# A fused attention and sine-gated feed-forward kernel on one Trainium2 core: the hand-held order of its 1816 steps is drawn up anew

## The chip, the cores and the metric

One core of one Trainium2 chip. The metric is the device time of one execution in microseconds (us), 381.02 as the median of three runs before the change (379.35, 381.02, 384.81). The engines are called by the profile's names: PE (TensorE; PEld its weight loads), ACT (ScalarE), DVE (VectorE), POOL (GpSimd) and SP (SyncE), which only issues transfers.

## The reference

Eight batches of eight heads, 576 positions of 64 values; then a feed-forward over the 4608 rows of 512.

```python
scores = q @ k.T / sqrt(64) + bias[bucket(|i - j|), head]
attn = exp(scores - max) / (sum + 1e-9)
x = (attn @ v).transpose(0, 2, 1, 3).reshape(4608, 512)
h = x @ w_in                       # 512 -> 2048
s = sin(alpha * h)
out = (h + s * s / (alpha + 1e-9)) @ w_out   # 2048 -> 512
```

## The kernel before, in words

The work is cut into 1816 named steps by `_graph` (L46 on), each with the engines that it may run on, what it depends on, how many of the eight PSUM banks it takes and which later steps free them. The text `ORDER` (from L343) lists all steps; `_planned` walks it, checks it and hands each step to an engine. Every engine runs its own steps in the order of that text and waits by semaphore for what a step needs. So the text alone sets each engine's queue, the banks and the choice of engine. A word is a step, then a slash with an engine's letter where it isn't the first choice (A ACT, D DVE, G POOL) and the bank number.

The names, with t a batch (0 to 7), p a pair of heads (0 to 3), b a block of 512 rows (0 to 8), f a 128-wide part of the 2048, and tau a tile of 128 output rows:

- `n` loads rows of q or k in fp16 on POOL (L581) and `t`, `c` turn them on PE (L703) and copy them (L653, L651), for batches 0 to 2. From batch 3 on `g` stages them in DRAM through POOL (L608) and `k` turns them with a transposing transfer on SP (L614).
- `v`, `y` load the value rows on POOL (L587, L593). For batch t they wait until every product with the values of batch t-2 is done, since two sets of buffers are used in turn.
- `T` is a score group of four matmuls (L766), `X..q`, `X..r` and `S` the scores of the last 64 positions (L749, L720, L725); `E..` is the exp on ACT (L774, L734) and `B..` the multiplication by the exp of the bias on DVE (L797, L779, L783, L740). There are 13 buffers for exps of `T` and 4 for those of `X`.
- `A` and `L` are the products with the values (L805, L810, L821); `N` and `NL` divide by the sums on DVE (L842, L843); `Y` and `YL` turn the result into the feed-forward's input xT, by PE for batch 0 (`P`, L868) and else by a transposing transfer on SP (L850, L861).
- `I` is the first feed-forward product, four 512-wide matmuls (L887), `Z` its sine on ACT (L893), `Q` the square on DVE or ACT (L900, L898), `G` the gate on DVE (L905), `O` two 512-wide matmuls of the second product (L915; the last tile goes in halves), `W` the eviction on DVE or ACT (L653, L651) and `D` the store on SP or ACT (L928).
- `j`, `m` load the bias pattern (L662, on SP or POOL) and cut its masks (L668, on POOL or DVE).

Block b's first product needs `Y` of all pairs of every batch that its rows touch. The order mixes batch t+1's attention with block t's feed-forward, so that PE has matmuls while ACT does exps. After the last exp, PE has some 20 us of `O` left.

Of the kernel before, what the change touches and what calls it, by code (L numbers as in the profile page):

```python
# [14 lines left out]
T, H, S, D = 8, 8, 576, 64  # L15
# [340 lines left out]
ET1100 P03/5 Y01 t120/4 BT1011 t210/7 ET1300 T1010/0 c120 L0/6 ET1010 Y03 wo0 t230/4 NL0 t200/5
T1311/2 c200 T1301/0 I0.8/6 ET1311 c230 ET1301 S1/5 c210 X11r/2 v10 I0.0/4 BT1000 EX11r BT1100 v13
I0.3/7 ES1 Z0.0 BS1 BT1010 I0.9/5 BT1300 PL0/3 I0.7/2 YL0 n211 Z0.9 Q0.0 I0.1/3 wo1 Z0.3 Q0.9 G0.0
Z0.7 I0.12/1 v21 Q0.3/A G0.9 I0.2/4 wo2 Z0.8 G0.3 Q0.7/A I0.5/5 n201 Q0.8 Z0.2 G0.7 I0.14/7 Z0.1
Q0.2 Q0.1/A G0.8 I0.10/2 Z0.12 wo3 G0.2 I0.13/6 Q0.12/A BX10r g31 G0.1 Z0.10 I0.4/4 BT1001 Z0.14  # L360
G0.12 A100/3 Q0.10/A Q0.14 I0.11/1 Z0.5 G0.10 g30 Z0.4 G0.14 I0.6/0 Q0.4/A BX11r Z0.11 N100
I0.15/7 G0.4 Q0.5/A y20 O0.0/3 Z0.6 G0.5 O1.0/2 g40 Q0.6/A O0.2 O0.4 Z0.15 G0.6 T1101/4 Z0.13 O1.2
Q0.11 ET1101 Q0.15 O0.6 G0.11 v22 A101/0 BT1301 O0.8 G0.15 A130/1 N101 O1.4 N130 Y10 O1.6 Q0.13
X11q/4 T1111/0 G0.13 t211/7 v20 ET1111 O1.8 c211 O0.10 y21 EX11q BT1111 T1200/0 O1.10 BT1311
ET1200 t201/7 t221/6 T1110/4 c221 T1201/0 ET1110 O1.12 BT1200 O1.14 ET1201 c201 O0.12 T1310/4 v23
W1 X10q/6 ET1310 T1210/0 BT1101 O0.14 BT1110 BX11q A110/2 BT1201 EX10q W0 A111/5 BT1310 D0 ET1210
N110 A120/4 N111 T1211/6 T2100/2 o2 T2110/0 ET1211 Y11 O3.0/5 BT1210 BX10q O3.2 ET2100 BT1211 O3.4
# [4 lines left out]
I1.1/7 Z1.5 g71 A210/6 I1.14/1 N210 Z1.8 NL1 I1.15/0 y31 Q1.8/A Q1.5 I1.0/6 G1.5 Z1.14 g50 Z1.1  # L372
I1.2/5 Q1.14 G1.8 Z1.0 I1.7/3 Q1.0/A BT2110 G1.14 v30 A220/2 G1.0 Z1.7 I1.13/1 g41 Q1.1/A N220
Z1.2 I1.6/6 G1.1 Q1.7/A Q1.2 I1.4/2 o3/A G1.7 Z1.6 I1.3/7 BT2000 Z1.4 G1.2 O2.12 Z1.15 O2.14 Q1.4
Q1.6/A I1.10/5 G1.4 g51 W2/A Q1.15 O5.0/3 Z1.3 G1.6 I1.12/4 Q1.3/A G1.15 Z1.13 I1.9/6 G1.3 Z1.10
O6.0/2 Q1.13 Z1.12 I1.11/7 G1.13 Z1.9 Q1.10 g60 X21q/0 Q1.9 Z1.11 O5.2 G1.10 EX21q O6.2 Q1.11 O5.4
BT2210 G1.9 A211/5 O5.6 G1.11 O6.4 BT2211 T2011/6 T2300/0 Q1.12 O6.6 ET2300 G1.12 O5.8 O6.8 N211
ET2011 O6.10 BT2010 Y21 BT2300 T2301/0 T2311/4 BT2011 T3110/6 O6.12 ET2311 BT2310 O5.10 BT2001
ET2301 O5.12 D2 O6.14 A200/5 ET3110 BT2301 O5.14 N200 W6/A T3300/0 YL1 T3011/6 W5 X20q/4 ET3300
# [601 lines left out]
```

## Time and profile before

| what | value |
|---|---|
| median of three runs | 381.02 us |
| the profiled execution | 381.76 us |
| its span, first to last instruction | 379.9 us |
| matmuls of PE | 3769 |
| first matmul starts | 3.85 us |

The profile's page gives the busy time of each engine, the span in 40 slices of 9.5 us (a digit is tenths; PEclk is the clock that TensorE was granted), and the chain of work that ended last. Of a row of stretches, the columns are its bounds, its length, the busy time of PE, PEld, DVE, ACT and POOL with counts, the granted clock, the DMA share and GB/s; where one engine alone was asked for, its busy time stands alone. A timeline row has the start, how long a merged piece lasts, the engine, line and operation, and in brackets the idle time before it with who ended it. A row of waits has the sum, the count and the longest. A matmul's own duration includes its latency; consecutive ones overlap, so a cost is read from starts.

### The profile page before, as it was taken

Reading aid. Unit: us, or ns where it says so; the run is one execution under the profiler, and the core shown is the slowest. Engines: PE = TensorE matmul, PEld = TensorE weight load, DVE = VectorE, ACT = ScalarE, POOL = GpSimd, SP = SyncE. Lnnn points to the kernel's source line nnn. Section 1 sums busy time; section 2 is a strip of 40 time slices with the busy share of each in tenths; the row PEclk is TensorE's granted clock in tenths of the full one; section 3 lists DMA queues with packets and bytes.
Section 4 is the critical chain, followed back from the end, with each engine's and each line's share of the span. In section 5 each row is a group of like instructions: output and inputs, shape, how many; then the busy total and the mean of one; then the engine's idle time right before and its main releaser. Section 6 shows DMA issues by size and latency. Waiting matters only on the chain.

```text
span 379.9 us, 9143 instructions
## 1 busy us (share of the span) xinstructions
PE 365.4 (96%) x3769; PEld 195.6 (51%) x3769; DVE 265.3 (70%) x613; ACT 310.5 (82%) x417; POOL 86.0 (23%) x104
## 2 busy tenths in 40 slices
PE   4879999999998899999999999999999999999996
PEld 3567445654464455544554555445654564444453
DVE  4789899639975496389754985596729866769412
ACT  5979998999899599899988989999899855686301
POOL 8894682048208000600000050500000000000000
PEclk9989999999999899999999999999999999999999
DMA  9999999999999992890254078980130032020005
GB/s 174 217 170 184 186 193 158 126 201 145 157 131 142 172 100 57 93 155 21 98 129 97 0 83 135 141 69 28 40 89 3 2 83 92 2 83 0 2 29 193
DMA packets 140889, 39.68 MB, mean 104 GB/s; under 512 B 126208, under 2 KB 136304, under 8 KB 140848
## 3 DMA queue, kind: packets, MB, share of 16 engines
q0 software_dynamic: 92864, 18.45, 60.0%
q1 hardware_dynamic: 46272, 18.61, 23.5%
q10 hardware_dynamic: 1712, 2.04, 1.6%
q8 instruction: 29, 0.48, 0.5%
q14 instruction: 12, 0.10, 0.1%
HBM read 36.89 MB, written 15.34 MB: 137 GB/s over the span
## 4 chain that ended last, share of the span: by engine, by line
PE 88%; DMA 6%; ACT 2%; POOL 1%; issue 1%; SPq 1%; DVE 1%; POOLq 0%
PE acc L915 33%; PE acc L887 31%; PE acc L810 8%; PE acc L766 8%; PE acc L805 2%; DMA xT<-xp 2%; DMA v<-in_v_dram 2%; PE acc L821 2%; DMA xT<-in_k_dram 2%; DMA toep<-e_sb 1%; ACT s L893 1%; PE acc L720 1%; PE acc L703 1%; POOL xT L581 1%; PE acc L749 1%
## 5 line engine op out<-in xcount | busy, mean ns | idle before, releaser
L915 PE MATMUL acc<-w_out,g 128*128 128x512 f16 (+1 forms) x592 | 144.3, 374 | 0.0
L887 PE MATMUL acc<-xT,w_in 128*128 128x512 f16 x576 | 135.8, 381 | 2.8 <-DMA xT<-xp 2.2
L774 ACT ACTIVATE u<-acc 128x1024 f16<-128x1024 f32 x128 | 123.7, 1034 | 12.2 <-PE acc L766 11.3
L893 ACT ACTIVATE s<-acc,alphaT 128x512 f16<-128x512 f32 x144 | 91.9, 682 | 23.6 <-PE acc L887 23.0
L905 DVE SCALAR_TENSOR_TENSOR g<-s,inv_a,acc 128x512 f16<-128x512 f16 x144 | 103.2, 742 | 7.3 <-ACT s L898 5.7
L887 PEld LDWEIGHTS <-w_in 128*128 128x128 f16 x576 | 55.3, 98 | 69.2 <-issue 6.5
L915 PEld LDWEIGHTS <-g 128*128 128x128 f16 x592 | 52.7, 98 | 59.0 <-issue 7.3
L797 DVE TENSOR_TENSOR u<-u,toep 128x256 f16<-128x256 f16 (+1 forms) x128 | 58.9, 489 | 19.8 <-ACT u L774 19.5
L587 POOL DMA_DIRECT2D v<-in_v_dram x32 | 30.9, 972 | 145.5 <-PE acc L821 79.0
L810 PE MATMUL acc<-v,u 128*128 128x65 f16 x1024 | 45.4, 196 | 0.5 <-DMA v<-in_v_dram 0.5
L900 DVE TENSOR_TENSOR s<-s 128x512 f16<-128x512 f16 x83 | 34.0, 419 | 17.0 <-ACT s L893 16.7
L810 PEld LDWEIGHTS <-u 128*128 128x128 f16 x1024 | 41.9, 99 | 4.9 <-issue 0.9
L766 PE MATMUL acc<-qT,kT 64*128 64x256 f16 x512 | 42.0, 278 | 1.5 <-DVE kT L653 1.0
L898 ACT ACTIVATE s<-s 128x512 f16<-128x512 f16 x61 | 37.9, 629 | 1.1
L653 DVE COPY outs<-acc 128x512 f32<-128x512 f32 (+1 forms) x24 | 16.2, 675 | 26.7 <-PE acc L915 25.4
L774 ACT ACTIVATE ux<-acc 128x1024 f16<-128x1024 f32 x32 | 32.4, 1035 | 1.8 <-PE acc L720 0.9
L766 PEld LDWEIGHTS <-kT 64*128 64x128 f16 x512 | 20.4, 96 | 22.8 <-issue 18.2
L842 DVE RECIPROCAL rden<-acc 128x4 f32<-128x4 f32 x72 | 12.7, 177 | 25.1 <-PE acc L810 18.7
L805 PE MATMUL acc<-vt,ux 128*128 128x130 f16 x128 | 28.8, 225 | 1.0 <-DMA vt<-in_v_dram 1.0
L843 DVE TENSOR_TENSOR xp<-acc,rden 128x256 f16<-128x256 f32 x64 | 27.2, 424 | 2.3
L651 ACT ACTIVATE outs<-acc 128x512 f32<-128x512 f32 (+1 forms) x13 | 7.6, 582 | 18.6 <-PE acc L915 18.5
L805 PEld LDWEIGHTS <-ux 128*128 128x128 f16 x128 | 12.7, 99 | 8.2 <-issue 2.8
(68 smaller groups left out, 199.2 us busy)
## 6 DMA issues: line engine op xcount, KB each, us to landing
out_dram<-outs SPq DMA_DIRECT2D x30, 256.0 KB, 2.3
v<-in_v_dram POOLq DMA_DIRECT2D x32, 128.0 KB, 6.8
staged_q<-in_q_dram POOLq DMA_DIRECT2D x5, 576.0 KB, 12.4
staged_k<-in_k_dram POOLq DMA_DIRECT2D x5, 576.0 KB, 14.9
w_in<-in_moe_w_in_dram POOLq DMA_DIRECT2D x4, 512.0 KB, 10.5
w_out<-in_moe_w_out_dram POOLq DMA_DIRECT2D x4, 512.0 KB, 10.6
xT<-in_q_dram POOLq DMA_DIRECT2D x11, 144.0 KB, 5.6
xT<-in_k_dram POOLq DMA_DIRECT2D x11, 144.0 KB, 5.9
```

Of the source, the lines that this page charges most:

```text
L587: self.nc.gpsimd.dma_start(out=self.vs[t % 2][:, c, :, 0:D], in_=src)
L766: self.nc.tensor.matmul(out=s[:, o:o + 256], lhsT=self.kT[t % 2][r, p, 128 * c:128 * c + 128], rhs=self.qT[t % 2][r, p, 256 * w:256 * w + ...
L774: self.nc.scalar.activation(out=c["u"], in_=c["s"], func=AF.Exp, scale=0.125)
L797: self.nc.vector.tensor_tensor(out=io, in0=io, in1=m, op=ALU.mult)
L805: nc.tensor.matmul(out=c["av"][:, 130 * j:130 * j + 130], lhsT=cx["u"][:, o:o + 128], rhs=vt[:, p, :], start=True, stop=True, skip_group_c ...
L810: nc.tensor.matmul(out=c["av"][:, 130 * j + 65 * a:130 * j + 65 * a + 65], lhsT=cells[ch // 2]["u"][:, o:o + 128], rhs=vv[:, ch, 2 * p + a ...
L887: self.nc.tensor.matmul(out=c["h"], lhsT=self.w_in[:, j, 128 * f:128 * f + 128], rhs=self.xT[:, j, 512 * b:512 * b + 512], start=(j == 0), ...
L893: self.nc.scalar.activation(out=c["s"], in_=c["h"], func=AF.Sin, scale=self.alphaT[:, f:f + 1])
L898: self.nc.scalar.activation(out=c["s"], in_=c["s"], func=AF.Square)
L900: self.nc.vector.tensor_tensor(out=c["s"], in0=c["s"], in1=c["s"], op=ALU.mult)
L905: self.nc.vector.scalar_tensor_tensor(out=self.g[b][:, f, :], in0=c["s"], scalar=self.inv_a[:, f:f + 1], in1=c["h"], op0=ALU.mult, op1=ALU ...
L915: self.nc.tensor.matmul(out=c["mo"], lhsT=self.g[b][:, f, 128 * (tau % 4):128 * (tau % 4) + 128], rhs=self.w_out[:, f, at], start=(f == 0) ...
```

## The change

The text `ORDER` is replaced; no other line differs, and each of the 1816 steps occurs in both. [...] What differs: the order on every engine, the banks, and some choices of engine. 44 squares go from DVE to ACT and 34 from ACT to DVE (on ACT 61 before, 71 after); of the evictions 10 go to ACT and 9 away (13 before, 14 after); stores on ACT's queue are 9 instead of 7; mask m0 goes from POOL to DVE; a few copies change sides. The table of ACT is changed between exp and sine 16 times in both. Core of the diff, with the places around the first product with values (A000), block 1's first product (I1.5, then I1.11) and block 2's (I2.0, then I2.14):

```diff
 ORDER = """
-id/A r00 ms r10/A r01 n011 r11/A sub n020 cst tab al n021 n100 f00 n031 th00/7 f10/A ch00 n010 f01
-th10/6 y00 th01/7 ch10 ch01/A T0000/0 v00 T0001/2 ET0000 n131 bu/7 ET0001 f11 t020/6 n030 be
...
-T0311/6 BX00r EX01q BT0011 A000/3 n210 BT0300 A010/2 EX00q n220 N000 A001/5 m3 BT0211 ET0311
...
-X20r/6 N120 ET2110 A131/3 S2/4 A121/2 EX20r N131 T2200/0 N121 O3.6 ES2 ET2200 BT2100 T2111/6 Y12
-T2101/2 O2.0/4 ET2111 O3.8 X21r/0 ET2101 O3.10 Y13 O3.12 EX21r O3.14 T2000/2 k30 T2201/6 T2211/0
-ET2000 O2.2 O2.4 ET2201 O2.6 O2.8 ET2211 BT2201 O2.10 BT2101 W3 T2001/2 T2210/6 T2010/0 BT2111
-ET2001 D3 L1/5 BT2200 ET2010 I1.5/3 BX21r D1 v33 BX20r ET2210 T2310/0 v32 k31 I1.8/2 ET2310 y30
...
-A221/2 BS2 BT2311 O4.0/3 EX20q N221 O4.2 BT3300 T3301/0 ET3011 T3000/4 Y22 A201/2 BX21q ET3301
...
-X31q/0 v31 T3111/4 O7.2 ET3111 Y20 g70 O7.4 O4.14 EX31q X30q/4 W4 T3201/6 O7.6 EX30q BT3011 k41
-S3/3 O7.8 g61 BT3000 ET3201 O7.10 BT3110 X31r/0 BX30r BX31q T3200/4 ES3 BT3001 EX31r T3010/6
-BT3111 I2.0/3 BT3201 v43 ET3010 A300/1 I2.14/0 ET3200 BT3010 BT3301 N300 I2.5/7 Z2.0 D6 BT3101
...
+id/A r00 ms r10/A r01 n011 r11/A sub n020 cst tab al n021 n010 f00 n030 th00/7 f10/A ch00 n131 f01
+th10/6 n031 th01/7 ch10/A ch01 T0000/0 y01 T0001/2 ET0000 t011/7 n100 f11/A bu/6 c011 v02 t020/5
...
+BT0101 t101/6 n200 ET0210 c110 T0311/0 T0110/4 n120 c101 A000/7 ET0311 m3 BT0210 A001/6 N000
...
+N121 T2311/4 EX21r T2211/6 BT2201 Y12 A131/1 BX11q ET2211 O3.10 N131 X21q/2 ET2311 T2100/6 Y13
+L1/1 EX21q O3.12 NL1 v32 k31 ET2100 O3.14 T2000/2 v20 W3 T2110/4 ET2000 T2101/6 S2/1 BT2211 v31
+I1.11/0 BT2311 ET2110 I1.12/3 g30 BT2210 BX21q ET2101 BT2300 D1 I1.9/2 BT2110 BX21r ES2 BT2200
...
+T3110/4 A201/6 Y21 ET3111 T3301/2 ET3110 v42 X30q/0 BT3111 O7.0/7 BT3010 g50 ET3301 O7.2 N201 O7.4
+BT3001 Y20 BX30r X31r/4 EX30q BT3110 BT3201 O4.0/6 BT3100 O7.6 EX31r T3300/0 D6 v41 T3210/2 ET3300
+T3101/4 g61 O4.2 ET3101 O4.4 BT3300 O7.8 BT3200 X31q/0 ET3210 T3011/4 O7.10 v43 ET3011 I2.14/3
...
 """
```

SP's queue around block 2 is, before: k30 D3 D1 k31 Y21 D2 YL1 Y22 k40 Y23 YL2 Y20 k41 D6; and after: D1 k30 D3 Y23 D0 Y22 YL1 k40 k41 D5 Y21 Y20 D6. POOL's queue begins, before, with 18 transfers of n, y, v and j ahead of v02, the last of batch 0's values; after, with 19 ahead of v01, the last there.

More of the change, by code (lines that the diff above doesn't have):

```diff
@@ L356 @@
[L356 to L367, printed above, removed]
@@ L374 @@
[L374 to L379, printed above, removed]
@@ new lines @@
+t131/6 c030 X00r/4 ET0111 n101 t100/1 c131 v00 t111/7 EX00r X00q/2 c111 v03 EX00q c100 T0211/4
+T0101/6 v01 m0/D ET0101 T0201/0 BT0011 X01r/2 n121 BT0111 ET0211 n201 BT0100 T0310/6 EX01r m1
+BT0000 t130/5 n231 ET0310 BX00r S0/4 BT0200 m2 T0210/2 c130 ET0201 wi1 t110/7 BT0010 BT0001 ES0
+BT0101 t101/6 n200 ET0210 c110 T0311/0 T0110/4 n120 c101 A000/7 ET0311 m3 BT0210 A001/6 N000
+ET0110 v12 T0301/0 N001 T0300/2 t121/7 ET0301 wi0 BT0310 X01q/4 BT0201 BX01r A010/6 BT0110 ET0300
+y11 BT0311 A020/1 n230 N010 EX01q A011/0 n220 BT0211 T1011/2 c121/A N011 T1100/4 A031/6 ET1011
@@ new lines @@
+O0.12 ET1211 W1 O0.14 X11q/0 ET2300 W0 t211/5 t210/3 A130/4 EX11q c210 T1310/6 BX10q T2210/2
+c211/A N130 A111/1 ET2210 BT1210 O3.0/0 N111 T2301/4 ET1310 T2201/2 BT1311 Y11 O3.2 BT1211 ET2301
+O3.4 A120/1 ET2201 BT2301 T2310/4 o2 T2200/6 O3.6 N120 ET2310 X21r/2 BT1310 A121/1 ET2200 O3.8
+N121 T2311/4 EX21r T2211/6 BT2201 Y12 A131/1 BX11q ET2211 O3.10 N131 X21q/2 ET2311 T2100/6 Y13
+L1/1 EX21q O3.12 NL1 v32 k31 ET2100 O3.14 T2000/2 v20 W3 T2110/4 ET2000 T2101/6 S2/1 BT2211 v31
+I1.11/0 BT2311 ET2110 I1.12/3 g30 BT2210 BX21q ET2101 BT2300 D1 I1.9/2 BT2110 BX21r ES2 BT2200
@@ new lines @@
+Z1.12 I1.6/7 y31 I1.1/6 v33 I1.8/1 Z1.1 Q1.12 v30 Z1.6 I1.5/5 Q1.1 g40 G1.12 Q1.6/A I1.14/4 Z1.5
+G1.1 Q1.5/A O2.0/3 BT2101 G1.6 O2.2 Z1.8 A220/6 BS2 y30 Z1.11 G1.5 I1.10/7 Q1.11/A Q1.8 N220
+I1.4/5 Z1.10 G1.11 Z1.14 O2.4 G1.8 I1.3/6 Q1.10/A BT2100 Z1.9 I1.0/1 Q1.14 Z1.3 G1.10 I1.13/0
+Q1.3/A k30 Q1.9 G1.14 I1.7/7 Z1.13 BT2310 G1.9 Z1.0 O2.6 G1.3 A230/4 Q1.13/A I1.2/2 Q1.0/A G1.13
+Z1.4 N230 I1.15/6 Z1.7 Q1.4 Z1.2 O2.8 G1.0 A231/4 Q1.2/A G1.4 D3 O2.10 Z1.15 N231 O2.12 Q1.15/A
+O6.0/5 G1.2 Q1.7/A X20r/0 O5.0/4 G1.7 EX20r A221/2 Y23 G1.15 O2.14 O6.2 N221 O6.4 W2 X20q/6 D0
@@ new lines @@
+T2011/0 T2001/2 EX20q O5.2 Y22 O6.6 ET2011 BX20q O5.4 O6.8 ET2001 o3 T2111/0 YL1 T2010/6 O5.6
+ET2010 L2/3 ET2111 X30r/6 NL2 k40 O6.10 EX30r BX20r T3201/0 BT2011 T3000/2 O6.12 BT2010 ET3000
+BT2111 O6.14 T3010/6 ET3201 BT3000 T3001/2 O5.8 k41 BT2001 ET3010 O5.10 W6 O5.12 BT2000 A210/5
+ET3001 O5.14 N210 S3/7 T3200/0 ES3 W5 T3100/2 A211/6 ET3200 BS3 D5 A200/7 ET3100 N211 T3111/0 N200
+T3110/4 A201/6 Y21 ET3111 T3301/2 ET3110 v42 X30q/0 BT3111 O7.0/7 BT3010 g50 ET3301 O7.2 N201 O7.4
+BT3001 Y20 BX30r X31r/4 EX30q BT3110 BT3201 O4.0/6 BT3100 O7.6 EX31r T3300/0 D6 v41 T3210/2 ET3300
@@ new lines @@
+A311/3 N310 Z2.8 X41r/0 O4.12 N311 EX41r O4.14 G2.6 O9.0/4 BT3301 O9.2 W4 O9.4 Q2.8 T3311/2 D4
+BX30q T3310/6 G2.8 A320/1 ET3311 BX31q YL2 O8.0/5 ET3310 N320 O8.2 S4/0 O8.4 ES4 BT3310 T3211/2
+T4000/0 T4301/6 ET3211 O9.6 Y31 O9.8 ET4000 O9.10 A330/3 ET4301 O8.6 N330 T4001/0 T4310/6 BT3211
+T4200/2 ET4001 O9.12 BT3311 O9.14 ET4200 A321/1 W9 O8.8 ET4310 N321 D9 T4300/2 T4311/0 ET4300
+T4011/6 A331/4 Y32 ET4011 O8.10 N331 O8.12 ET4311 BT4200 T4210/2 Y33 T4201/6 BT4011 L3/4 ET4201
+BT4000 T4211/0 k50 y51 ET4210 NL3 T4010/6 O8.14 v53 ET4211 X40r/2 I3.11/4 y41 ET4010 BT4211 y40
@@ L460 @@
+O31.10 O34.4 O33.8 O30.14 O29.8 W30 O28.10 O33.10 D30/A O31.12 O31.14 O28.12 W31 O35.0b/4 O34.6
+D31/A O35.0a/6 O34.8 O28.14 O35.4b W28 O35.8b O33.12 D28 O34.10 O29.10 O35.12b O29.12 W35b/A O32.6
+D35b O33.14 O29.14 W33 O32.8 W29/A O32.10 D33 D29/A O34.12 O32.12 O34.14 O32.14 W34/A O35.4a D34/A
+W32 O35.8a O35.12a D32 W35a/A D35a/A
 """
```

166 lines of the change are left out of this document (79 added, 87 removed).

## The prediction

> **What bounds the kernel now.** I read the page first, then the waits of TensorE, then the stretches around its two stalls.
>
> ```profile
> PE 365.4 (96%) x3769; PEld 195.6 (51%) x3769; DVE 265.3 (70%) x613; ACT 310.5 (82%) x417; POOL 86.0 (23%) x104
> ...
> PEclk9989999999999899999999999999999999999999
> DMA  9999999999999992890254078980130032020005
> ...
> PE 88%; DMA 6%; ACT 2%; POOL 1%; issue 1%; SPq 1%; DVE 1%; POOLq 0%
> ```
> ```profile
> PE acc L887 <- DMA xT<-xp: 2.2, 1, 2.2
> PE acc L805 <- DMA vt<-in_v_dram: 1.0, 1, 1.0
> PE acc L766 <- DVE kT L653: 1.0, 2, 0.8
> ...
> PE acc L887 <- issue: 0.6, 1, 0.6
> PE acc L810 <- DMA v<-in_v_dram: 0.5, 1, 0.5
> ```
> ```profile
> 122.00:125.00 3.00, 0.84 (x10) 0.42 (x9) 1.49 (x5) 2.98 (x5) 1.82 (x2) 1.00 1.38 108
> 125.00:128.50 3.50, 3.50 (x26) 1.99 (x24) 1.17 (x4) 1.88 (x2) 0.00 (x0) 0.51 1.74 128
> ...
> 19.20:22.70 3.50, 1.44 (x43) 0.95 (x43) 3.50 (x9) 3.50 (x5) 3.33 (x8) 1.00 1.45 175
> 22.70:26.10 3.40, 3.40 (x61) 3.31 (x61) 2.52 (x7) 1.23 (x2) 3.23 (x7) 0.50 1.14 158
> ```
>
> TensorE is busy 96% of the span and carries 88% of the chain. The change neither adds nor removes a product, so it can only win back stalls, and these are small: the five waits above sum to 5.3 us. Two stand for most of what can be moved. At 122 us TensorE is idle for 2.2 us (0.84 busy of 3.00) and in the next 3.5 us its clock is 0.51, which loses another 0.49 x 3.5 = 1.7: 3.9 us at one place. Around 21 us it waits for the value rows (1.0 + 0.5), and 3.4 us at clock 0.50 follow: 1.7 more.
>
> **Part 1, the order of the transposed rows on SyncE (-3.6 us).** Why was the transposed row late at 122 us?
>
> ```profile
> 110.01 1.19 SPq L850 DMA_TRANSPOSE xT<-xp  x1
> 111.31 2.98 SPq L614 DMA_TRANSPOSE kT<-staged_k  x1
> 114.38 1.22 SPq L850 DMA_TRANSPOSE xT<-xp  x1
> 115.70 2.46 SPq L861 DMA_TRANSPOSE xT<-xl  x2
> 118.21 1.26 SPq L850 DMA_TRANSPOSE xT<-xp  x1
> 119.57 4.58 SPq L614 DMA_TRANSPOSE qT<-staged_q  x1
> ```
> ```profile
> L850 SPq DMA_TRANSPOSE xT<-xp x28: 1188/1206/2107, 59.6 to 311.6; - x28
> ...
> DMA to landing us min/median/max: 2.4/2.5/7.3
> ```
> ```profile
> L842 DVE RECIPROCAL rden<-acc 128x4 f32<-128x4 f32 x72 | 12.7, 177 | 25.1 <-PE acc L810 18.7
> L843 DVE TENSOR_TENSOR xp<-acc,rden 128x256 f16<-128x256 f32 x64 | 27.2, 424 | 2.3
> ```
> ```profile
> 124.66 1.50 PE L887 MATMUL acc<-xT,w_in 128*128 128x512 f16 x4 [2.16 <-DMA xT<-xp]
> ```
> The piece of 118.21 is Y20, which I2.0 waits for. Ahead of it on SyncE stood the transposes k40, Y23 and YL2; and where the median landing is 2.5 us after the issue, I2.0 could start only at 124.66, 6.4 after it. In the new order k40 and k41 stand well ahead, and only Y21 stands between them and Y20. From the last product by v (A201) to the first product of block 2 (now I2.14) TensorE has 9 moe-out pieces (18 matmuls), 5 score groups, two X..q and one X..r group. Their prices:
>
> ```profile
> 342.00:361.00 19.00, 19.00 (x89) 8.60 (x88) 13.10 (x25) 9.40 (x16) 0.00 (x0) 1.00 0.00 1
> ...
> 20.09 0.41 PE L749 MATMUL acc<-qT,kT 64*128 64x64 f16 x16 [0.29 <-DVE qT L653]
> ...
> 28.69 0.39 PE L766 MATMUL acc<-qT,kT 64*128 64x256 f16 x4
> 29.01 0.31 PE L725 MATMUL acc<-qT,kT 64*64 64x64 f16 x8
> 29.25 0.70 PE L703 MATMUL acc<-ident,xT 96*64 96x96 f16 x24
> ```
> ```profile
> 80.27 0.74 PE acc L821 x34
> ```
> A 128x512 matmul costs 19.00/89 = 0.213; a score group 0.32 (28.69 to 29.01); an X..q 0.41; an X..r two 512-wide matmuls, 0.43. Sum 18 x 0.213 + 5 x 0.32 + 0.82 + 0.43 = 6.7 us of cover. Against it: 0.177 + 0.424 for the division plus some 0.1 to start, then 2.5 (quiet) to 7.3 (worst): 3.2 to 8.0. I take 7.0, near the slow end, because k41 and the first of batch 4's loads may overlap it: a stall of 0.3, and no slow clock. Gain 3.6; bounds 3.9 and, at 8.0 (idle 1.3), 2.6 or, if the clock then falls, 0.9.
>
> **Part 2, the same cover elsewhere (+0.5 us).** The new order cuts it. Block 1 begins 3.7 us after A131 (3 moe-out pieces 1.28, 4 score groups 1.28, X21q 0.41, L1 0.74, and S2, four matmuls of 64 columns) where before 8.7 us lay between A121 and I1.5. Priced alike, the shortest covers of blocks 3 to 7 go from 8.2, 5.2, 5.6, 6.1, 4.8 to 3.7, 3.9, 4.4, 4.3, 4.6. The need on a quiet queue is 3.2, or 4.4 where another transpose's 1.2 of issue stands just ahead. So each holds by a hair: I charge some 0.1 a block, 0.5 in all. Ends: 0, and for a landing of 7.3 at block 1 an idle time of 4.3 and a slow stretch of 1.7.
>
> **Part 3, the head (-0.4 us).**
>
> ```profile
> 21.76 0.23 PE L805 MATMUL acc<-vt,ux 128*128 128x130 f16 x1 [1.04 <-DMA vt<-in_v_dram]
> ...
> 22.59 0.45 PE L810 MATMUL acc<-v,u 128*128 128x65 f16 x6 [0.54 <-DMA v<-in_v_dram]
> ```
> ```profile
> L581 POOL DMA_DIRECT2D xT<-in_q_dram x11 | 7.3, 661 | 1.7 <-POOLq L965 0.8 <-DMA w_in<-in_moe_w_in_dram 0.6
> ...
> L668 POOL COPY mt<-toep 64x192 f16<-64x192 f16 x8 | 3.1, 388 | 0.3
> ```
> A000 starts when the last of batch 0's value rows lands, 22.6 before. It is now the 20th load on GpSimd's queue and was the 19th, by one row load: up to 0.66 later. In the wait TensorE now does more ahead of A000: one score group, S0 (0.31) and two turns (0.70) more, X01q (0.41) less: 0.9 us. Net -0.9 to +0.5 with the rest unmoved; I take -0.4. Mask m0 goes to VectorE, 2 x 0.39 by GpSimd's row; the value rows cover it, and if they land earlier it is paid once, 0.8. The slow clock at 22.7 I leave: TensorE is still idle more than half of the stretch ahead of it.
>
> **Part 4, ScalarE and VectorE (+0.5 us).**
>
> ```profile
> L774 ACT ACTIVATE u<-acc 128x1024 f16<-128x1024 f32 x128 | 123.7, 1034 | 12.2 <-PE acc L766 11.3
> L893 ACT ACTIVATE s<-acc,alphaT 128x512 f16<-128x512 f32 x144 | 91.9, 682 | 23.6 <-PE acc L887 23.0
> ...
> L900 DVE TENSOR_TENSOR s<-s 128x512 f16<-128x512 f16 x83 | 34.0, 419 | 17.0 <-ACT s L893 16.7
> ...
> L898 ACT ACTIVATE s<-s 128x512 f16<-128x512 f16 x61 | 37.9, 629 | 1.1
> ```
> ```profile
> 90.00:100.00 10.00, 9.91 (x18) 1.00 2.45 157
> ```
> Squares on ScalarE go from 61 to 71: 10 x 0.629 = 6.3 us more there, 10 x 0.419 = 4.2 less on VectorE. Over the span both have room (82% and 70%), so TensorE's work hides it; but until about 120 us ScalarE is nearly full (9.91 of 10.00). Counted in the written order from block 0's first product to block 2's, ScalarE's work is now 95% of TensorE's and was 92%. Score groups whose banks wait for an exp stand with less behind them, so a few waits of some tenths come: I take 0.5, bounds 0 and 3. Evictions (13 to 14 on ScalarE) and two stores moved to its queue cost nothing beside the last block's matmuls; without that cover, one eviction. Table loads stay at 16. Value loads of batches 2, 4 and 5 now stand behind loads that wait for an older batch's last product; counted by their order each still lands 3 us or more ahead of its use, and a lost cover is paid one for one.
>
> **Sum.** -3.6 + 0.5 - 0.4 + 0.5 = -3.0. The profiled execution took 381.76 (span 379.9 and 1.9 around it), so 378.8. That execution stands 0.7 above the median of the runs shown, 381.02, which range from 379.35 to 384.81. Faster or slower by under 2% of the median (373.4 to 388.6) is about what a measurement of this kernel can tell from no change, so I forecast no change that counts.
>
> **Rivals.** (a) My sum: 378.8, by itself 376 to 381. Chance 0.45.
> (b) Slower: the cut cover fails at block 1. The worst landing, 7.3, with 0.7 ahead of it makes 8.0 against 3.7: 4.3 idle and 1.7 of slow clock instead of the 0.1 charged, 378.8 + 5.9 = 384.7. It is slower than before from an extra loss of 3.0, that is from a landing of 4.4 or more with the slow clock. For it: SyncE's landings spread from 2.4 to 7.3, and block 1 falls in the first 145 us, where the page shows the DMA engines 9 tenths busy. Against: GpSimd's streams ahead of block 1 should end about then, as the next loads wait for L1. Chance 0.20. [...]
> (c) The change doesn't do what it says: stalls move but as many come, 381.8 within 1. Chance 0.13. For it: five tight covers and the tight banks could return 3 us in tenths.
> (d) The head stays at full clock as well: 1.7 less, 377.1. Chance 0.10, since ScalarE still paces the first 20 us.
> (e) The slow stretch at 125 us comes without the idle time, so only 1.9 of the 3.6 is gained: 380.5. Against it, both slow stretches follow a stretch with TensorE busy under half (1.44 of 3.50, 0.84 of 3.00). Chance 0.07. [...]
> (f) A queue blocks behind a load in the new order, as (b) at two blocks: over 388.6. Chance 0.05.
>
> **Numbers.** The likeliest is 378.8. With one in ten left out on each side the range is 375 to 386. Faster by over 2%: 0.03 (the far end of (d)); slower: 0.07 ((f) and the end of (b)); within 2%: 0.90.
>
> **What would show it.** Right: no idle TensorE over 0.5 us ahead of block 2's first product and no second slow stretch; covers at blocks 1 and 3 to 7 that end within 0.3 us; A000 not before 22.6. Wrong: a wait of L887 for xT over 1 us at any block, a clock below 1.00 after 30 us, or waits of TensorE for ScalarE that sum to over 2 us.

## The result, and the profile after

The kernel after took 381.74 us (median of 20 runs, 379.51 to 384.35), the kernel before 379.83 (20 runs in the same session, 378.20 to 384.81). The ratio is 1.0050, with a 95% interval from 1.0029 to 1.0071: 1.9 us slower, where 3.0 us less was forecast. By the 2% line it is no change, as forecast, and 381.7 lies within the wide range of 375 to 386; the likeliest time, 378.8, was missed by 2.9. Two later sessions gave 1.0014 (.9981 to 1.0047) and 1.0020 (.9995 to 1.0045), whose intervals include 1.

The profiled execution of after took 381.75, with a span of 380.0. The first thing to see is that the profiled execution of before, 381.76, was not typical: it stands 1.9 above the median of its 20 runs. The sum was made against it. Of the page of after, in the order of the lines shown of before:

```profile
PE 365.6 (96%) x3769; PEld 195.8 (52%) x3769; DVE 264.2 (70%) x607; ACT 315.4 (83%) x425; POOL 85.3 (22%) x102
...
PEclk9989999999999999999999999999999999999999
...
PE 78%; ACT 7%; DMA 5%; DVE 5%; issue 3%; POOL 2%; POOLq 0%; DVEq 0%; ACTq 0%
```

TensorE does as much as before, but the chain that ended last goes through it for 78% of the span and no longer for 88%; ScalarE and VectorE have 12% and had 3%. The second slow digit of the clock, at 125 us, is gone. The waits of TensorE (sum, times, longest):

```profile
...
PE acc L703 <- issue: 1.3, 1, 1.3
PE acc L703 <- ACT u L774: 1.0, 2, 0.5
PE acc L805 <- DVE kT L653: 0.9, 1, 0.9
...
PE acc L766 <- ACT ux L774: 0.6, 2, 0.4
PE acc L887 <- DMA xT<-xp: 0.6, 2, 0.3
```

The wait of 2.2 us for xT is gone, and in its place stand many of some tenths, and one of 1.3 that no semaphore ended. Four stretches of after, two of the head and two of block 2 (length; busy time of PE, PEld, DVE, ACT, POOL; granted clock; DMA share; GB/s):

```profile
20.00:24.00 4.00, 2.01 (x36) 1.35 (x36) 3.24 (x9) 3.93 (x5) 3.81 (x9) 0.95 1.57 154
24.00:28.00 4.00, 3.98 (x75) 3.35 (x75) 2.99 (x11) 2.02 (x3) 3.90 (x7) 0.63 1.06 156
120.00:124.00 4.00, 4.00 (x39) 1.71 (x37) 1.58 (x3) 4.00 (x5) 4.00 (x4) 1.00 1.60 160
124.00:128.00 4.00, 4.00 (x36) 2.11 (x35) 2.26 (x6) 3.94 (x6) 2.24 (x2) 1.00 2.40 152
```

Block 2 is as forecast: TensorE is busy throughout, at full clock. The head is not: TensorE is busy half of the time from 20 to 24 us, its clock then falls, and ScalarE, which was full, is left with half its work. The clock column counts slow stretches from the trace's first record of the clock on (the last section has what lies ahead of it).

To see where time goes I use a lag: the start of TensorE's work near a time, less the time that all its work ahead of that would take at the spacings of an undisturbed stretch. What it grows by between two times is lost there.

| profiled execution | 41 us | 110 us | 130 us | end |
|---|---|---|---|---|
| before, the one of the prediction | 12.6 | 13.2 | 17.1 | 18.6 |
| before, again (first experiment) | 12.1 | 12.8 | 14.9 | 16.5 |
| after | 14.5 | 15.4 | 15.8 | 19.2 |
| after, again | 13.7 | 14.6 | 15.0 | 18.0 |
| after, a third time | 14.3 | 15.2 | 15.6 | 19.1 |

Between the first row and the third: head +1.9, to 110 us +0.3, block 2 -3.5, the rest +1.9; and by those spacings TensorE's own work is 0.6 less in the new order, an estimate. That sums to zero, as the two spans do (379.9 and 380.0). Against the second row block 2 is worth only 1.7.

### The profile page after: what moved, and what is told of

Same layout as the page of the kernel before. It is cut to its first block, busy times and chain, and to the rows that moved or that the text cites. A ratio compares the mean times of both kernels' runs of the same rounds, so it can differ in the third digit from the quotient of the medians.

```text
span 380.0 us, 9151 instructions
## 1 busy us (share of the span) xinstructions
PE 365.6 (96%) x3769; PEld 195.8 (52%) x3769; DVE 264.2 (70%) x607; ACT 315.4 (83%) x425; POOL 85.3 (22%) x102
## 4 chain that ended last, share of the span: by engine, by line
PE 78%; ACT 7%; DMA 5%; DVE 5%; issue 3%; POOL 2%; POOLq 0%; DVEq 0%; ACTq 0%
PE acc L915 31%; PE acc L887 25%; PE acc L766 7%; PE acc L810 7%; ACT s L893 3%; DMA xT<-xp 2%; PE acc L805 2%; DVE g L905 2%; DMA vt<-in_v_dram 2%; DMA xT<-in_k_dram 2%; PE acc L720 1%; PE acc L749 1%; ACT u L774 1%; PE acc L821 1%; ACT s L898 1%
## 5 line engine op out<-in xcount | busy, mean ns | idle before, releaser
L887 PE MATMUL acc<-xT,w_in 128*128 128x512 f16 x576 | 133.6, 379 | 1.0 <-DMA xT<-xp 0.6
L905 DVE SCALAR_TENSOR_TENSOR g<-s,inv_a,acc 128x512 f16<-128x512 f16 x144 | 103.0, 743 | 12.8 <-ACT s L898 11.4
L893 ACT ACTIVATE s<-acc,alphaT 128x512 f16<-128x512 f32 x144 | 93.0, 682 | 19.2 <-PE acc L887 16.3
L797 DVE TENSOR_TENSOR u<-u,toep 128x256 f16<-128x256 f16 (+1 forms) x128 | 58.1, 484 | 10.5 <-ACT u L774 10.2
L587 POOL DMA_DIRECT2D v<-in_v_dram x32 | 32.2, 1034 | 120.6 <-PE acc L821 86.9
L766 PE MATMUL acc<-qT,kT 64*128 64x256 f16 x512 | 43.7, 280 | 2.5 <-ACT ux L774 0.6
L898 ACT ACTIVATE s<-s 128x512 f16<-128x512 f16 x71 | 43.6, 627 | 1.2
L810 PEld LDWEIGHTS <-u 128*128 128x128 f16 x1024 | 41.1, 98 | 5.6 <-issue 0.9
L900 DVE TENSOR_TENSOR s<-s 128x512 f16<-128x512 f16 x73 | 30.2, 420 | 18.4 <-ACT s L893 18.3
L766 PEld LDWEIGHTS <-kT 64*128 64x128 f16 x512 | 20.8, 96 | 24.2 <-issue 20.5
L653 DVE COPY outs<-acc 128x512 f32<-128x512 f32 x23 | 15.8, 688 | 19.1 <-PE acc L915 19.1
L593 POOL DMA_DIRECT2D vt<-in_v_dram x16 | 13.9, 877 | 29.5 <-PE acc L821 28.5
```

What stands on the lines that cost most here:

```text
L587: self.nc.gpsimd.dma_start(out=self.vs[t % 2][:, c, :, 0:D], in_=src)
L766: self.nc.tensor.matmul(out=s[:, o:o + 256], lhsT=self.kT[t % 2][r, p, 128 * c:128 * c + 128], rhs=self.qT[t % 2][r, p, 256 * w:256 * w + ...
L797: self.nc.vector.tensor_tensor(out=io, in0=io, in1=m, op=ALU.mult)
L810: nc.tensor.matmul(out=c["av"][:, 130 * j + 65 * a:130 * j + 65 * a + 65], lhsT=cells[ch // 2]["u"][:, o:o + 128], rhs=vv[:, ch, 2 * p + a ...
L887: self.nc.tensor.matmul(out=c["h"], lhsT=self.w_in[:, j, 128 * f:128 * f + 128], rhs=self.xT[:, j, 512 * b:512 * b + 512], start=(j == 0), ...
L893: self.nc.scalar.activation(out=c["s"], in_=c["h"], func=AF.Sin, scale=self.alphaT[:, f:f + 1])
```

## The experiments

The theories by their names in the expectations. A: the profiled executions are typical, and block 2 gains what they show. B: the stall of before at block 2 was special to its execution. H: the head of after is what loses. All ratios are to the kernel before on the same chip in the same session, with 95% intervals.

**The kernel before, unchanged.**

> The kernel before, unchanged. Theory A (the two profiled executions are typical): its profile shows again about 2 us of TensorE idle and a stretch at about half clock near 125 us (mean clock .991), and its time is at 380-382. Theory B (the wait at block 2 in the profiled execution of before was longer than in most runs): median near 379.8, and its new profile has the idle at the second block's xT transposes (line 887, near 122 us) at 1.5 us or less, or no half-clock stretch at 125 us (clock .995 or more). Ratio to before 1.000 either way.

Measured: 380.03, ratio 1.0008 (.9978 to 1.0038). Its profile has the wait, but no slow clock:

```profile
124.08 1.02 PE L887 MATMUL acc<-xT,w_in 128*128 128x512 f16 x4 [2.00 <-DMA xT<-xp]
```

Neither theory as written: the wait is in both profiles (2.2 and 2.0), the slow stretch behind it in one. The list of runs gives each run's mean clock, and one stretch of 3.41 us at half clock takes .0045 off it (half of 3.41, over 379). Of 149 runs of before in five sessions 79 have a clock of .998 or more, 42 about .995, 27 about .991 and one .987. So the execution that the prediction was made on, with two such stretches (.991), is of a kind that came in 27 of 149.

**Row 20 early.** The kernel before with Y20 right behind N201.

```diff
-N201 k40 A231/6
+N201 Y20 k40 A231/6
...
-ET3111 Y20 g70
+ET3111 g70
```

> The kernel before with one move: the block-2 row 20 is transposed right behind N201 (as after has it, 7 us earlier in SyncE's queue), the K cast k40 behind it. Nothing else changes. Theory A: the wait of 2.2 us at block 2 and the slow stretch behind it go, time 3 to 3.6 us below the kernel before (ratio .991 to .993). Theory B: in most runs little of it is there, 0 to 1.5 us (ratio .996 to 1.000). Rival (c) of the prediction, a next row comes late instead: 0, with a wait on another row near 122 us.

Measured: 379.67, ratio .9981 (.9955 to 1.0008): theory B's size. But its profile is 2.2 shorter than that of before again, with a lag that grows by only 0.3 at block 2. Row 23 now landed 0.25 after TensorE began the group, whose fourth matmul reads it, and cost nothing; the value rows v31 landed 0.25 after TensorE came for them. In other runs something had to be later; the experiment with rows 20 and 23 shows what.

**Three spliced orders.** The head of after up to the first gate products (BT1011) with the order of before behind it; after up to block 2 (I2.8) with before behind it; before up to W0, near 68 us, with after behind it.

```diff
 c200 t231/7 EX11r BT1011
-I0.2/5 c231 I0.3/4 Z0.2 BT1301 c220
+n210 c231 v11 n221 c220 t210/7 T1311/2 I0.8/0
```

> Order of after up to the first gate matmuls (about 40 us), order of before from there; one PSUM bank of I0.8 differs. Theory A and B alike: the head of after costs +1.9 us, seen as TensorE idle of 1.3 to 1.5 us ahead of the second or third gate group near 40 us (instruction supply: no semaphore ended it) and 0.5 to 0.7 more near 34 us; ratio 1.004 to 1.006 against before. Rival (the head's loss was of that one execution, or is paid back at block 1, where before also has slack): 0 to +0.5 us, ratio 1.000 to 1.001.

> Order of after up to block 2's gate group I2.8 (about 130 us), order of before for the rest; three PSUM banks differ. Theory A: it keeps the head's loss (+1.9) and the gain at block 2 (-3.3), and saves the 2.0 us that after loses behind 130 us: 2 us below after, 1.4 below the profiled execution of before; ratio to before .996 to 1.000. Theory B: the gain at block 2 is 0 to 1.5, so it stands 0.4 to 1.9 above before: ratio 1.001 to 1.005. If the second half of after is not slower than that of before, it stands level with after (1.005).

> Order of before up to W0 (the end of the turns into block 1's outputs, near 84 us; both kernels have nearly the same work behind them there, 8 tasks differ), order of after from there. Theory H (the head of after costs 2.4 us of its 1.9 in all: after stands 14.5 behind at 41 us, the repeated kernel before 12.1): 2.4 us below after, ratio to before .998 to 1.000, and a mean clock of 1.0 in most runs as before has. Rival S (the head's loss is paid anyway, the second half alone decides): level with after, 1.004 to 1.006.

Measured: 393.07, ratio 1.0346 (1.0302 to 1.0389); 386.14, 1.0163 (1.0128 to 1.0198); 383.87, 1.0097 (1.0060 to 1.0133). All three miss every expectation, and for a reason of their own. In the first TensorE stands at the seam:

```profile
47.56 0.69 PE L703 MATMUL acc<-ident,xT 96*64 96x96 f16 x12 [6.67 <-DMA xT<-in_k_dram]
```

The order of before goes on with the turn t210; its rows n210 are the last that after loads, so in the splice they are issued only at the seam. In the second, TensorE waits 2.95 for a division at 146 us; in the third, three times for ScalarE and once for VectorE between 68 and 81 us, 2.3 in all, though the finished steps differ by only eight each way at the seam. An order is tuned to its own queues: a splice measures the seam. So the parts were tested by single moves from here on.

**Rows 20 and 23 early.** As above, with k40 behind both.

```diff
-N201 k40 A231/6
+N201 Y20 A231/6
...
-ET3001 Y23 T3101/0 NL2
+ET3001 Y23 k40 T3101/0 NL2
```

> The kernel before with rows 20 and 23 of block 2 both issued as soon as their norms are done, the K cast k40 behind both (in the last experiment k40 stayed ahead of row 23, which then landed 0.25 us after TensorE came for it). Theory A: the idle of 2.1 us at block 2 goes in every run: ratio .993 to .996. Theory B' (the idle is paid back later or lost to something else in most runs): ratio .997 to 1.000, though the idle at line 887 near 122 us is under 0.3 us in the profile.

Measured: 378.47, ratio .9970 (.9939 to 1.0000). The ratio is that of theory B'. The wait for xT is gone, and another stands in its place:

```profile
123.70 0.37 PE L810 MATMUL acc<-v,u 128*128 128x65 f16 x7 [1.69 <-DMA v<-in_v_dram]
```

These are the value rows v31. Before issues them on POOL at 117 us, behind three other loads; after issues them at 81 us.

**v31 alone, and all three.** v31 loaded right behind v32, by itself, then with rows 20 and 23 early, which was run twice.

```diff
-T2310/0 v32 k31
+T2310/0 v32 v31 k31
...
-X31q/0 v31 T3111/4
+X31q/0 T3111/4
```

> The kernel before with the value rows v31 alone loaded early, row 20 left late. Theory A (two late transfers behind each other): TensorE still waits about 2 us for row 20 near 122 us, ratio .999 to 1.001. Rival (v31's load is what delays row 20: both run at 118 to 124 us): row 20 lands 1.5 us or more earlier and the wait shrinks to 0.5 us or less, ratio .994 to .997.

> The kernel before with rows 20 and 23 early (as in the last experiment) and the value rows v31, for which TensorE then waited 1.85 us at the same place, loaded right behind v32 (37 us earlier). Theory A (two late transfers hid behind each other at block 2): TensorE's idle between 120 and 130 us falls under 0.4 us in the profile, ratio .993 to .996. Rival (a third transfer is late there as well): idle of 1.5 to 2 us again, ratio .997 to 1.000.

> The kernel before with rows 20 and 23 and v31 early, once more for its interval: ratio .987 to .995 (it measured .9897, from .9861 to .9933, on six runs; by its profile alone, 2.1 us of wait less, .9945). Rival (the earlier six runs were lucky): .996 to 1.000.

Measured: v31 alone 378.36, ratio .9971 (.9940 to 1.0002), with TensorE still waiting for xT; all three 376.98, .9897 (.9861 to .9933), and 377.34, .9924 (.9895 to .9953). First v31 alone, then all three:

```profile
123.49 1.86 PE L887 MATMUL acc<-xT,w_in 128*128 128x512 f16 x4 [2.28 <-DMA xT<-xp]
```
```profile
120.00:124.00 4.00, 4.00 (x41) 2.20 (x41) 2.95 (x11) 3.98 (x6) 1.06 (x2) 1.00 2.53 153
124.00:128.00 4.00, 4.00 (x35) 2.16 (x34) 3.40 (x9) 3.83 (x7) 0.00 (x0) 1.00 1.61 138
```

Theory A, with its cause corrected: at block 2 two transfers are late, and in the profiles the wait goes only with both. The gain is 3.9 and 2.9 us by the two ratios, more than the 2.1 of the wait. The slow stretch behind it isn't the reason: runs of .998 or more alone give 3.2 and 2.6 (376.6 against 379.8 and 377.0 against 379.6), so the excess stays open. This kernel beats both before and after.

The times don't show that one move alone brings nothing. The two ratios of a single repair, .9970 and .9971, multiply to .9941, which lies inside the second interval. And v31 alone splits: its seven runs of .998 or more average 377.6, which is 2.0 below such runs of before, and its five others 380.6. The profile is of one of those five, with a slow stretch behind the wait. So the rival, that loading v31 late is what delays row 20, is open for the other seven, of which no profile was taken.

**The head: turns later.** After, with two of the five turns ahead of its first gate products behind the first two of them.

```diff
-c201 t220/2 ET1301 X11r/0 y10 c200 t231/7 EX11r BT1011 I0.2/5 c231 I0.3/4 Z0.2
+c201 ET1301 X11r/0 y10 c200 EX11r BT1011 I0.2/5 I0.3/4 t231/7 c231 t220/2 Z0.2
```

> The kernel after, with two of the five 12-matmul turns of its head (t231, t220) and their copy c231 moved behind the first two gate groups I0.2 and I0.3. [...] Rival (a fixed wait at this place, for data or a semaphore): the idle stays 1.2 or more, now ahead of or within I0.2, and the ratio stays 1.004 to 1.006.

Measured: 382.20, ratio 1.0058 (1.0033 to 1.0082): the rival's ratio, but not its idle time. After first, then this kernel:

```profile
39.53 0.27 PE L703 MATMUL acc<-ident,xT 96*64 96x96 f16 x3
41.12 0.40 PE L703 MATMUL acc<-ident,xT 96*64 96x96 f16 x9 [1.31 <-issue]
```
```profile
40.43 1.89 PE L887 MATMUL acc<-xT,w_in 128*128 128x512 f16 x8 [0.30 <-ACT u L774]
42.24 0.70 PE L703 MATMUL acc<-ident,xT 96*64 96x96 f16 x24
43.54 1.67 PE L887 MATMUL acc<-xT,w_in 128*128 128x512 f16 x7 [0.60 <-DVE qT L653]
```

The wait that no semaphore ended, 1.31 us in after, isn't left there, but no time is gained: waits for VectorE's copies of the moved turns (0.60) and for ScalarE (0.30) take its place.

**The head: masks early.** After, with m1 and m2 ahead of three row loads on POOL.

```diff
-X01r/2 n121 BT0111 ET0211 n201 BT0100 T0310/6 EX01r m1 BT0000 t130/5 n231 ET0310 BX00r S0/4 BT0200 m2
+X01r/2 m1 m2 n121 BT0111 ET0211 n201 BT0100 T0310/6 EX01r BT0000 t130/5 n231 ET0310 BX00r S0/4 BT0200
```

> The kernel after, with the mask copies m1 and m2 moved ahead of three row loads (n121, n201, n231) in GpSimd's queue. In after m1 ends at 21.10 because two load issues of 0.7 us stand ahead of it; VectorE waits 0.76 us for it, its copy of kT for the next turn is late by that, and TensorE waits 0.90 us at A000. Theory M: that wait falls by 0.7, the busy share between 20.1 and 23.6 us rises from .56 to about .75, fewer runs get the half-clock window: 0.7 to 1.5 below after, ratio to before 1.001 to 1.003. Rival (ScalarE's queue of u decides at this place): 0 to 0.3, ratio 1.004 to 1.006, half-clock window in as many runs.

Measured: 380.79, ratio .9996 (.9969 to 1.0022), so its time lies below that of after, but not by M's cause. VectorE no longer waits for the mask, yet TensorE's wait at A000 is what it was:

```profile
24.64 0.27 PE L805 MATMUL acc<-vt,ux 128*128 128x130 f16 x1 [0.90 <-DVE kT L653]
```

VectorE and ScalarE are both busy 4.00 of 4.00 us from 20 to 24 there. M falls; a half-clock stretch came in 10 of the 12 runs.

**The head: TensorE kept busy.** After, with 16 matmuls of batch 0's scores done again into the same banks, where TensorE waits anyway.

```diff
+_AGAIN = {(0, 2, 1, 0): 2, (0, 3, 1, 1): 2, (0, 1, 1, 0): 3}
...
-        for ci in (1, 0):
+        for ci in (1, 0) * _AGAIN.get((t, p, w, half), 1):
```

> The kernel after, with 16 matmuls of block 0 done again (the score tiles T0210 and T0311 twice, T0110 three times: the same values into the same banks, 1.7 us of TensorE work at full clock) where TensorE waits for ScalarE and VectorE between 20 and 24 us anyway. Theory C (with only about 2.1 of 4 us busy between 20 and 24 us, TensorE gets half the clock from about 23.5 to 27 us, feeds ScalarE late there, and ScalarE bounds the head): the clock stays at 1.0 in most runs, ScalarE is busy 3.5 of 4 us or more between 24 and 28 us (2.0 and 2.5 in the two profiles of after), time 1 to 2 us below after, ratio to before .9985 to 1.001. Rival (the waits themselves cost, the clock does not): the clock is full and the time that of after, 1.002 to 1.005, or up to 1.7 us longer.

Measured: 380.86, ratio 1.0009 (.9984 to 1.0033). The clock obeys: 8 of 12 runs at .998 or more, against 3 of the 44 runs of after. These eight average 380.2, the other four took 381.0, 381.4, 383.0 and 386.7. The profiled run was one of the four; the stretch at full clock is shown below, by the kernel that has this edit and other work ahead of blocks 5 and 6.

**The second half: other work ahead of block 5 and block 6.** After, with X61r moved ahead of I5.3 and O22.4 ahead of I6.2; then this with the masks, and with the repeated matmuls.

```diff
-O19.14 y70 ET6101 I5.3/6 y60 W19 v63 D16 X61r/0
+O19.14 y70 ET6101 X61r/0 I5.3/6 y60 W19 v63 D16
...
-BX71r I6.2/5 BT7001
+BX71r O22.4 I6.2/5 BT7001
...
-Q6.9/A O22.4 Z6.1
+Q6.9/A Z6.1
```

> The kernel after with one piece of other TensorE work (X61r, 0.6 us; O22.4, 0.43 us) put ahead of the first gate group of block 5 and of block 6. Theory L (the two waits for xT of .46 and .47 us are part of the second half's loss): 0.6 to 0.9 below after, ratio to before 1.0025 to 1.0035. Rival (the wait moves to ScalarE's or VectorE's next piece): 0 to 0.3 below after, ratio 1.004 to 1.005.

> The kernel after with both repairs: m1 and m2 early, and a piece of other work ahead of the first gate groups of blocks 5 and 6. If the two losses are separate places of one chain they add: 0.7 to 1.5 and 0.6 to 0.9 below after, ratio to before .998 to 1.0015. If one hides the other: 1.0015 to 1.003.

> The kernel after with the matmuls of block 0 done again (as in the run before this one) and a piece of other work ahead of the gate groups of blocks 5 and 6. If the head's clock and the two late waits for xT are separate losses, both come off: 2 to 3 us below after, ratio to before .996 to .999. If the head's clock brings nothing: 1.001 to 1.003.

Measured: 380.87, ratio 1.0016 (.9989 to 1.0043); with the masks 381.27, 1.0021 (.9998 to 1.0044); with the repeated matmuls 379.92, .9994 (.9969 to 1.0018). The first gate group in after, then in the first of these kernels:

```profile
L887 PE MATMUL acc<-xT,w_in 128*128 128x512 f16 x576 | 133.6, 379 | 1.0 <-DMA xT<-xp 0.6
```
```profile
L887 PE MATMUL acc<-xT,w_in 128*128 128x512 f16 x576 | 133.4, 379 | 0.3 <-DVE outs L653 0.2
```

The two waits go; .7 us of idle time at this line, as L expects. The time shows no gain by it: 1.0016 is below L's range, but stands between the two later measurements of after (1.0014 and 1.0020). With the repeated matmuls 11 of 12 runs are at full clock. Its head, to be held against the first two rows of after above:

```profile
20.00:24.00 4.00, 2.90 (x65) 2.46 (x61) 3.38 (x9) 4.00 (x6) 3.86 (x8) 1.00 1.47 159
24.00:28.00 4.00, 4.00 (x119) 3.60 (x116) 3.87 (x14) 3.62 (x5) 3.90 (x7) 1.00 1.06 153
```

TensorE at full clock hands ScalarE 3.62 us of work from 24 to 28, where it had 2.02. The time lies between the two forecasts (.996 to .999 and 1.001 to 1.003), and its interval wholly below that of the first measurement of after (1.0029 on), but not below those of the two later ones. That of the run with the masks alone does so too, without a cause, which shows how far such times can be trusted.

**All three repairs, and after a third time.**

> The kernel after with three repairs: matmuls of block 0 done again between 20 and 24 us (clock), the turns t231 and t220 behind the first two gate groups (the wait of 0.6 to 1.8 us near 40 us in which TensorE waits for nothing that a semaphore shows), other work ahead of the gate groups of blocks 5 and 6. If that wait is a loss of its own beside the other two: another 1 to 1.5 us below the last kernel with two repairs (.9994), ratio .995 to .997. If the time is given back behind it, as in the run that moved the turns alone (1.0058): .999 to 1.002.

> The kernel after, unchanged, a third time, for its interval (1.0050, from 1.0029 to 1.0071, and 1.0014, from .9981 to 1.0047): 1.002 to 1.006, clock below .998 in 9 of 12 runs or more; the head at 41 us 1.5 to 3 us further behind than the 11 to 12 that the kernel before shows in its undisturbed profiles.

> The kernel after, unchanged, as a control on this chip. Theory: its losses are set by its order and come in every run: ratio to before 1.003 to 1.007; its new profile shows again a half-clock window near 23 us (clock .996 or less in 8 of 10 runs), TensorE waits for ScalarE's u and VectorE's kT of 2 us in all between 19 and 24 us, and the two xT waits near 237 and 277 us. Rival (chance of one execution): at least two of these are gone and the ratio is near 1.000.

Measured: the three repairs 380.61, ratio 1.0007 (.9984 to 1.0031), no better than two (.9994), as forecast for the case that the time won at 39 us is given back behind it; the run with the turns alone had shown the same. After again: 1.0014, below its expectation, and 1.0020, within it (intervals at the head of this text). Their profiles have the slow stretch near 23 us, ScalarE's gap behind it, and the wait at 39 us; the waits for xT at blocks 5 and 6 are in the third (0.6 in all) and shorter than 0.2 in the second. After again, and before again for comparison:

```profile
20.00:24.00 4.00, 2.14 (x48) 1.62 (x45) 4.00 (x10) 4.00 (x6) 3.90 (x7) 0.93 1.78 174
24.00:28.00 4.00, 4.00 (x78) 3.42 (x78) 2.99 (x11) 2.49 (x4) 3.90 (x8) 0.65 1.15 177
34.00:40.00 6.00, 5.31 (x135) 3.50 (x130) 4.76 (x13) 6.00 (x9) 3.96 (x6) 1.00 1.58 192
40.00:46.00 6.00, 5.69 (x36) 2.80 (x37) 5.45 (x12) 4.79 (x8) 2.77 (x4) 1.00 1.50 196
```
```profile
20.00:24.00 4.00, 2.96 (x79) 2.27 (x79) 4.00 (x10) 4.00 (x5) 3.83 (x8) 1.00 1.36 171
24.00:28.00 4.00, 3.59 (x91) 2.87 (x88) 3.90 (x12) 4.00 (x6) 3.83 (x9) 1.00 1.05 156
34.00:40.00 6.00, 5.20 (x121) 3.28 (x120) 5.96 (x12) 4.79 (x6) 1.93 (x3) 1.00 1.40 197
40.00:46.00 6.00, 6.00 (x30) 2.80 (x31) 3.97 (x10) 5.87 (x9) 4.42 (x6) 1.00 1.76 185
```

## Why the prediction was wrong, point by point

**The base.** The sum was set against an execution with two slow stretches. The runs give their price: the 79 runs of before at full clock average 379.63, the 42 with one stretch 380.77, the 27 with two 381.93, so 1.1 and 1.2 each. "The slow clock at 22.7 I leave" took for part of the kernel what 53% of its runs don't have. From the median of the 20 runs the same -3.0 would have given 376.8; measured were 381.7, so the terms were off by 4.9 against a typical run and by 3.0 against the profiled one.

**Part 1, block 2 (-3.6): right in size against that execution, half wrong in cause.** The wait and the slow stretch are gone in every profile of after, and mending this place alone in before gained 3.9 and 2.9. Against before again, which has no slow stretch there, the lag gives 1.7 only: from a typical run the base and this term are one error. But "in the new order k40 and k41 stand well ahead" names one of two late transfers. Moving row 20 alone gained 0.2% (.9981, to 1.0008); v31 lands at nearly the same moment (123.8, row 20 at 124.0 in before again), and that after issues v31 36 us earlier was not priced. Here rival (c), that stalls move, was true of a smaller change than the one made.

**Part 3, the head (-0.4): the step that failed.** It let A000 wait for the value rows, counted the cover ahead of A000 and one load more on POOL, and took the slow clock as given. Measured, A000 comes at 24.0, 24.0 and 24.6 us in the three profiles of after and at 21.8 and 22.7 in the two of before, and in after it waits for VectorE's copy of a turn:

```profile
24.02 0.27 PE L805 MATMUL acc<-vt,ux 128*128 128x130 f16 x1 [0.90 <-DVE kT L653]
```

The lag at 41 us is 13.7 to 14.5 in after and 12.1 and 12.6 in before: about +1.8 where -0.4 was forecast. From 20 to 24 us TensorE is busy 2.01, 2.14 and 2.91 of 4 in the three profiles of after, and the clock falls in each (0.63, 0.65 and 0.68 from 24 to 28 us); before again has 2.96 and keeps it (1.00). In 41 of 44 runs of after at least one slow stretch comes, in 70 of 149 of before. At half clock TensorE feeds ScalarE late (2.02, 2.49 and 2.90 us of work from 24 to 28 us, against 4.00). With the prices of before for each clock the runs of after would average (3 x 379.63 + 31 x 380.77 + 10 x 381.93)/44 = 380.96, against 380.40 for before: 0.6 of the 1.1 by which these runs differ (381.52 and 380.40). That the new order loses the clock more often, and that filling the gaps keeps it, is shown by the runs at .998 or more (3 of 44 of after, 8 and 11 of 12 with the repeated matmuls); the time that they brought, 0.1 to 0.4% against the three measurements of after, is no larger than the intervals.

By which path the head loses is not shown. At 34 us the lag of after is no more than 0.6 above that of before; most of the loss falls between 34 and 41 us. TensorE's waits of over 0.15 us from 34 to 46 us are, in after, only such as no semaphore ended (1.74, 0.95 and 1.31 in the three profiles, 0.62 and 0.81 in the two of before), and none is for ScalarE. In the full-clock profile shown above this wait ends at 38.4, in the three of after at 40.3 to 41.1. So a slow clock may cost time by bringing TensorE late to this point; no run tests it.

**Part 2, cut covers (+0.5), and Part 4, ScalarE and VectorE (+0.5): right in kind, too small.** Covers "hold by a hair" was right: blocks 5 and 6 missed by 0.3 and 0.3 of idle time, the others held. From 130 us to the end the lag grows by 3.0 to 3.5 in after and by 1.5 and 1.6 in before: 1.4 to 2.0 more, where 1.0 was charged for both parts. Of TensorE's time from 132 to 320 us, after and before again:

```profile
132.00:320.00 188.00, 186.87 (x1904) 98.80 (x1903) 137.03 (x319) 170.42 (x229) 20.03 (x22) 1.00 0.61 81
```
```profile
132.00:320.00 188.00, 187.95 (x1909) 99.25 (x1906) 134.86 (x317) 165.64 (x221) 15.90 (x20) 1.00 0.53 77
```

1.13 idle against 0.05 (0.68 and 1.10 in the other two profiles of after), and ScalarE 4.8 us fuller. That waits for banks are the rest is not shown.

**The rivals.** (b), block 1's cover, didn't come: it held with 0.6 to spare in after. (e) has it the other way round: the idle time is in both profiles of before, the slow stretch in one. (c), that stalls move but as many come, 381.8 within 1, is what was measured, at a chance of 0.13; but its reason, tight covers and banks, accounts only for what was lost behind 130 us. No rival had the head lose; that was missing. Of the signs, block 2 showed all that was to show the sum right, and no wait for xT came over 1 us; of those of being wrong one came, the waits for ScalarE of over 2 us: 2.8, 3.7 and 1.4 in the three profiles of after, all ahead of 24 us, and 1.1 and 1.7 in the two of before.

**What stays open.** By the lag the terms are -1.7 to -3.5 at block 2, +1.8 in the head, +0.2 to 110 us and +1.4 to +2.0 behind 130 us, with 0.6 less work: -0.7 to +1.7, beside the +0.5 to +1.9 of the three sessions. How the loss divides between the head and the second half rests on these profiles; no pair of times here separates the two, as each repair brings 0.1 to 0.5% at intervals of 0.25%.

## What to carry to other kernels

Before a sum is made against a profile, look where its execution stands among the runs, and take a half-clock stretch in it as a chance and not as part of the kernel (70 of 149 runs of before had one). Where a late transfer is moved, look for another on a second queue that is due at the same point: the wait may pass to it (2.0 us for row 20 became 1.69 for v31). When a whole order is drawn up anew, the stretch where TensorE is half idle while ScalarE is full deserves the closest look, for the clock can fall there, and ScalarE then gets its work late (in after TensorE was busy 2.01 and ScalarE 3.93 of 4 us, then the clock was 0.63 and ScalarE's work 2.02).

## What the runs showed of the hardware

- The stretches at half clock last 3.41 us in the profiles of before (from 22.67 and from 125.07 us) and of after (from 23.56). With the turns later the clock is 0.86 from 20 to 24 us and 0.50 from 24 to 28, which is longer than one such stretch. They are at no fixed place in the program: before again has none, at a mean clock of 1.000. Nor does the busy share of TensorE ahead of them part the profiles. With the masks early it is busy 2.57 of 4 us from 20 to 24, and the clock is 0.57 from 24 to 28; with the three repairs of after it is busy 2.60, and the clock stays at 1.00. Waits of 2.16 and 2.28 us at block 2 were followed by a slow stretch (0.51 from 125 to 128.5 in before, 0.64 from 124 to 128 with v31 alone), waits of 2.00 and 1.69 were not (1.00 in before again and with rows 20 and 23 early). What decides it is not shown.
- The trace's first record of the clock comes 12.43 us after the start in before and 13.32 in after, and the clock column gives 1.00 ahead of it. But there a score matmul (L766) lasts 0.42 us, and 0.27 at full clock behind it (medians of both profiles), so TensorE runs slower there.
- In 15 of the 20 profiles a wait of TensorE that no semaphore ended ends between 37 and 42 us, 0.2 to 1.8 long; behind 46 us none shows one of 0.2 or more. The two runs in which two turns stand later are among the five without it. The trace also has 29 transfers of the kind instruction, 0.48 MB in all. In before one lands at 37.67 us, and such a wait ends at 39.18; in after they land at 33.41 and 39.60, and such waits end at 34.92 and 41.12: 1.5 us later each time. No such wait follows the other landings of these two profiles. That TensorE waits for these transfers is not shown beyond this.

```profile
q8 instruction: 29, 0.48, 0.5%
```
